# Two gates and a second norm's scale and shift, computed as column-tiled row products in a transformer block on Trainium2

## The chip, the cores and the metric

The kernel runs on one core of one Trainium2 chip. The metric is the device time of one execution, in microseconds (us). The engines are TensorE (PE, with its weight loads PEld), VectorE (DVE), ScalarE (ACT), GpSimd (POOL) and SyncE (SP), which issues nearly all DMAs.

## What is computed

The reference is a transformer block with adaptive layer norm. Six vectors of 1024 come out of one product of the conditioning vector `c` with `w_mod`; they scale, shift and gate an attention part (32 heads of 32, one shared key and value head) and a SwiGLU feed-forward part. There are 2048 tokens, D = 1024, F = 3584, all in bf16.

```python
mod = (_silu(c) @ w_mod).reshape(c.shape[0], 6, 1, -1)
sa, ca, ga, sb, cb, gb = (mod[:, 0], mod[:, 1], ..., mod[:, 5])
h = _layernorm(x) * (1 + ca) + sa
x = x + ga * A(h, wq, wk, wv, wo)     # attention, one k and v head for 32 q heads
h = _layernorm(x) * (1 + cb) + sb
x = x + gb * B(h, w1, w3, w2)         # (silu(h @ w1) * (h @ w3)) @ w2
```

The change is about the last four of the six vectors: `ga` (m = 2), `sb` (m = 3), `cb` (m = 4) and `gb` (m = 5). The first two are needed first and are computed by other code (L769), which stays.

## The kernel before

The kernel writes all its work as nodes of a graph (`G.add`, with the engine, what is read and written, an assumed duration and a priority). A planner, `schedule`, then walks through assumed time and lays down a fixed order of instructions for each engine. Where several kinds of work are possible, the table `CH` (number of the decision: alternative taken) says which comes first. Semaphore waits follow from the graph. Each engine works through its list strictly in order, so one instruction that waits holds up everything behind it on its engine.

The work runs in these stages.

1. The head: `x` is loaded in 16 tiles of 128 tokens, normalised on DVE (`ln`, L573 to L616) and transposed on PE (L630). The first norm's scale is multiplied into the weights: `kscale` and `qscale` (L798, L804, L807) make scaled key and query weights. `QCUT` cuts the query weights into three parts; the part k = 1 is scaled in eight pieces, of which every second goes to ACT when `QACT` is 1:

```python
if k == 1 and c % 2 < QACT:
    G.add("act", lambda e, c=c: e.activation(WQ[:, c, a:b], WO[:, c, a:b], ACT.Identity, ...   # L804
else:
    G.add("dve", lambda e, c=c: e.tensor_scalar(WQ[:, c, a:b], WO[:, c, a:b], ...              # L807
```

   The raw query weights lie in the buffer `WO` until they are scaled; then the output weights are loaded into it (L875). Key, value and query projections are `kproj` (L685, L692), `vproj` (L699, L702) and `qproj` (L709, copied out by L712).

2. Attention runs over eight blocks of 256 queries. In each, one unit of work is eight score matmuls (L969) of 32 rows each into half of PSUM (six banks, `SP`) and two exponentials on ACT of 128x1024 (L979). DVE sums the exponentials in trees (L996, L1002, L1012), PE multiplies them with V (L1035) and forms the denominators (L1062), DVE copies these out (L1074, L1083, L1086) and divides (L1092 to L1102).

3. After block 0, and then after each block, `post` does the output projection (L1167), the second norm, and the feed-forward: gate and up matmuls (L1208), tanh on ACT (L1216), products on DVE (L1213, L1223, L1228), the down projection (L1279, and L1250 in the last block). The feed-forward of one block is laid between the scores of the next. Its weights pass through a ring of six buffers in `WREG`, `HREG` and `X`.

The four vectors fall into stage 2, during the first block's attention, when the rest of the query projections is the only other work for PE. `vec(m, key, out)` loads the 1024 columns of `w_mod` that belong to m in four pieces of 512 KB (512 rows by 512 columns, L893) through three slots `WMS`, which lie in `WREG`. For each 128x128 tile it loads the weights into PE and multiplies by one column of the conditioning vector `SCT` (L899): 64 matmuls of one column for each vector. The vector thus comes out with one element per partition, which is what the second norm's scale and shift need (`MODC`, copied by L907). A gate is needed along the free axis in all partitions: `gate(m)` transposes it on PE (L914), copies it (L916), writes it to DRAM (L918) and reads it back broadcast to all partitions into `GBB` (L920). The first gate is then multiplied into the output weights (L926). The second gate goes into the same `GBB` and is used in the feed-forward.

After a few marks of time without work PE fills in with dummy matmuls (L1320, up to 250 us of planned time), which the planner adds.

Of the kernel before, what the change touches and what calls it, by code (L numbers as in the profile page):

```python
# [8 lines left out]
P = 128  # L9
# [4 lines left out]
LOOK = 0.5  # L14
LK = 0.6
LF = 0.5
CH = {2: 1, 24: 1, 25: 2, 82: 1, 136: 1, 142: 1, 147: 1, 188: 1, 202: 1, 210: 1, 211: 1, 232: 1, 242: 1, 374: 1,
      412: 1, 414: 1, 429: 1, 431: 1, 495: 1, 516: 1, 573: 1, 632: 1, 801: 2, 807: 1, 1116: 2, 1191: 1, 1204: 1,
      1208: 2, 1236: 1, 1333: 2, 1726: 2, 1801: 1, 1814: 1, 1818: 2, 1846: 1, 1943: 2, 2336: 2, 2411: 1, 2424: 1,
      2428: 2, 2456: 1, 2553: 2, 2946: 2, 3021: 1, 3034: 1, 3038: 2, 3066: 1, 3163: 2, 3556: 2, 3631: 1, 3655: 1,  # L20
      3669: 1, 3689: 1, 3778: 2, 3793: 1, 3802: 1, 4131: 1, 4166: 1, 4167: 1, 4183: 2, 4192: 3, 4238: 1, 4302: 1,
      4387: 1, 4394: 1, 4418: 1, 4429: 2, 4475: 1, 4490: 1, 4508: 2}


class Node:
# [390 lines left out]
def build(nc, x_in, wq_in, wk_in, wv_in, wo_in, w1_in, w3_in, w2_in, c_in, wmod_in, out, S, D, F):  # L416
# [51 lines left out]
    DSB = sb("DSB", [P, 2, QB], F32)  # L468
    ASB = XN[:, 2:4, :].rearrange("p a d -> p (a d)").bitcast(F32).rearrange("p (a q) -> p a q", a=4)
    SCT = sb("SCT", [P, NC], BF16)  # L470
    GC = sb("GC", [P, 2, NC], BF16)
    GR = sb("GR", [8, 2, P], BF16)
    gscr = nc.dram_tensor("gscr", [2, D], BF16, kind="Internal").ap()
    CROW = sb("CROW", [8, P], BF16)
    CT = sb("CT", [8, P], F32)
    SCR = sb("SCR", [8, P], BF16)
# [46 lines left out]
    def grp(allow=None):  # L523
        g = Group()
        g.allow = allow
        return g
# [16 lines left out]
    def dma(fn, key, reads=(), writes=(), nbytes=0, after=(), clear=()):  # L543
        return G.add("sp", fn, reads=reads, writes=writes, dur=0.06, dkey=key, nbytes=nbytes, after=after, clear=clear)
# [175 lines left out]
    ONPOOL = ()  # L720
    ME = True
    KP = 1
    QACT = 1
    TRP = 1
    EV = (("act",), ("act", "dve"), ("dve",), ("dve",))
    ORDER = ("x0", "x1", "x2", "x3", "x4", "x5", "a0", "a1", "x6", "a2", "a3", "x7", "a4", "a5", "a6", "a7", "q0",
# [38 lines left out]
    for h in (1, 0):  # L765
        for k in range(NC):
            def mm(e, k=k, g=gm[h], h=h):
                for j in range(NC):
                    i = e.matmul(PB[g.bank][:, j:j + 1], WM01[:, k, h * D + j * P:h * D + (j + 1) * P], SCT[:, k:k + 1],  # L769
                                 start=(k == 0 and j == 0), stop=True, skip_group_check=True)  # L770
                return i
# [108 lines left out]
        qproj(256, 256, f, (0, 1))  # L880

    def wms(i):
        return [("WMS", i)]
    nwm = [0]

    def vec(m, key, out):
        g = grp()
        for h in range(2):
            for kb in range(2):
                sl = nwm[0] % 3  # L890
                nwm[0] += 1
                c0 = m * D + h * 512
                dma(lambda e, kb=kb, c0=c0, sl=sl: e.dma_start(  # L893
                    WMS[:, sl], wmod_in[kb * 512:(kb + 1) * 512, c0:c0 + 512].rearrange("(c p) f -> p c f", p=P)),
                    ("wms", sl), writes=wms(sl), nbytes=P * 2048 * 2, after=[wo_load])
                for k in range(4):
                    def mm(e, kb=kb, h=h, sl=sl, g=g, k=k):
                        for j in range(4):
                            i = e.matmul(PB[g.bank][:, h * 4 + j:h * 4 + j + 1], WMS[:, sl, k, j * P:(j + 1) * P],  # L899
                                         SCT[:, kb * 4 + k:kb * 4 + k + 1],  # L900
                                         start=(h == 0 and kb == 0 and k == 0 and j == 0), stop=True,
                                         skip_group_check=True)
                        return i
                    G.add("pe", mm, reads=["SCT"] + wms(sl), dur=4 * 0.034, lat=0.2,
                          acq=g if (h == 0 and kb == 0 and k == 0) else None, groups=[(g, "w")], mode="F")
        a, b2 = {2: (1.0, 0.0), 3: (1.0, 0.0), 4: (1.0, 1.0), 5: (0.5, 0.0)}[m]
        G.add("dve", lambda e, g=g: e.tensor_scalar(out, PB[g.bank][:, 0:8], a, b2, ALU.mult, ALU.add),  # L907
              writes=[key], groups=[(g, "r")], dur=0.15, prio=4 if m in (3, 4) else 0)

    def gate(m):  # L910
        i = m // 3
        vec(m, ("GC", i), GC[:, i])
        g = grp()
        G.add("pe", lambda e, g=g, i=i: e.transpose(PBH[g.bank][0:8, 0:P], GC[:, i], IDENT[:]),  # L914
              reads=["IDENT", ("GC", i)], dur=0.07, lat=0.2, acq=g, groups=[(g, "w")], mode="F")
        G.add("dve", lambda e, g=g, i=i: e.tensor_copy(GR[:, i], PBH[g.bank][0:8, 0:P]), writes=[("GR", i)],  # L916
              groups=[(g, "r")], dur=0.2, prio=0)
        dma(lambda e, i=i: e.dma_start(gscr[i].rearrange("(k p) -> k p", p=P), GR[:, i]), ("gw", i), reads=[("GR", i)],  # L918
            writes=[("GSCR", i)], nbytes=2048)
        dma(lambda e, i=i: e.dma_start(GBB[:], gscr[i].unsqueeze(0).broadcast_to([P, D])), ("gr", i),  # L920
            reads=[("GSCR", i)], writes=[("GBB", 0), ("GBB", 1)], nbytes=P * D * 2)

    G.chain = GCH
    gate(2)
    for f in range(NC):
        G.add("dve", lambda e, f=f: e.tensor_tensor(WO[:, f, :], WO[:, f, :], GBB[:], ALU.mult),  # L926
              reads=["WO", ("GBB", 0), ("GBB", 1)], writes=[("WOG", f)], dur=dve_t(1024, 2), prio=6)
    for m in (3, 4):
        vec(m, ("MODC", m), MODC[:, m, :])
    gate(5)  # L930
    G.chain = 0
    for tb in range(1, NTB):
        for f in range(NC):
# [434 lines left out]
```

## Time and profile before

| | us |
|---|---|
| median of 4 runs | 1135.64 |
| lowest, highest | 1133.03, 1136.79 |
| the profiled execution, its own time | 1133.43 |
| the profiled execution, its span from first to last instruction | 1131.6 |

| engine | busy us | share of the span |
|---|---|---|
| PE | 1104.4 | 98% |
| DVE | 995.5 | 88% |
| ACT | 1020.1 | 90% |
| POOL | 36.7 | 3% |

| group of lines in the profile | count | mean ns of one |
|---|---|---|
| L979 exponential, ACT | 1024 | 1111 |
| L1216 tanh, ACT | 112 | 720 |
| L969 score matmul, PE | 4096 | 273 |
| L1035 product with V, PE | 4096 | 274 |

All durations in the document are those of one profiled execution. Neighbouring instructions of one engine overlap in the profile, since each is shown from its start to its result, so the distance from start to start is shorter than a duration. Busy time of PE is no proof that PE is at its limit: a matmul of 256 columns is shown with 273 ns, and the next can start 109 ns after it. The mean granted TensorE clock was 0.998 of full speed.

### The profile page before, as it was taken

How to read it: one execution, taken by the hardware profiler on the slowest of the kernel's cores; microseconds unless marked ns; L12 is line 12 of the kernel's file. 1: busy time of each engine (PE TensorE's matmuls, PEld its weight loads, DVE VectorE, ACT ScalarE, POOL GpSimd, SP SyncE). 2: the span in 40 equal slices, each digit the busy share in tenths (PEclk: the TensorE clock that was granted, in tenths of full speed). 3: DMA queues.
4: the chain of work that ended last, by engine and by line, in shares of the span. 5: the costliest groups of instructions: out<-in, count | busy, mean ns of one | idle time of the engine just before them, and what ended most of it. 6: DMA issues, size and time to landing. Idle time of an engine off the chain costs nothing.

```text
span 1131.6 us, 34956 instructions
## 1 busy us (share of the span) xinstructions
PE 1104.4 (98%) x15531; PEld 744.3 (66%) x15566; DVE 995.5 (88%) x1504; ACT 1020.1 (90%) x1167; POOL 36.7 (3%) x86
## 2 busy tenths in 40 slices
PE   7898999999999999999999999999999999999998
PEld 4564444767577757776677757776677757777883
DVE  6878899999989998999999998999999999997552
ACT  5999999999999999999999999999999999991110
POOL 3200000000000000000000000000000010000000
PEclk9999999999999999999999999999999999999999
DMA  9706203966596658766696649756785659656994
GB/s 332 230 25 188 76 1 88 285 192 176 142 259 195 168 163 217 213 185 178 147 258 184 182 123 261 206 170 173 170 249 171 178 140 271 191 166 182 295 309 142
DMA packets 378854, 211.58 MB, mean 187 GB/s; under 512 B 21840, under 2 KB 369488, under 8 KB 378704
## 3 DMA queue, kind: packets, MB, share of 16 engines
q1 hardware_dynamic: 376624, 209.22, 66.4%
q8 instruction: 122, 2.00, 0.8%
q10 hardware_dynamic: 2080, 0.13, 0.1%
q14 instruction: 28, 0.23, 0.1%
HBM read 201.98 MB, written 4.20 MB: 182 GB/s over the span
## 4 chain that ended last, share of the span: by engine, by line
PE 85%; ACT 8%; DVE 4%; SPq 1%; DMA 1%; issue 0%; POOL 0%; DVEq 0%
PE PB L1208 34%; PE PB L1279 14%; PE SP L969 13%; PE PB L1035 9%; ACT UREG L979 8%; PE PB L1167 4%; PE SP L1208 3%; PE PB L709 2%; PE SP L1279 2%; PE PB L1062 1%; PE PB L1250 1%; PE SP L1250 1%; DMA WO<-in_A_wq_dram 1%; SPq L751 1%; DVE UREG L996 1%; DVE UREG L1012 1%
## 5 line engine op out<-in xcount | busy, mean ns | idle before, releaser
L979 ACT ACTIVATE UREG<-SP 128x1024 bf16<-128x1024 f32 x1024 | 965.1, 1111 | 1.3 <-PE SP L969 0.7
L1002 DVE TENSOR_TENSOR UREG<-UREG 128x2048 bf16<-128x2048 bf16 x248 | 301.8, 1217 | 1.5 <-ACT UREG L979 0.3
L969 PE MATMUL SP<-QT,KT 32*128 32x256 bf16 x4096 | 203.8, 273 | 5.3 <-ACT UREG L979 3.6
L1208 PE MATMUL PB<-QT,WREG 128*128 128x256 bf16 x1648 | 206.8, 273 | 0.5 <-DVE GSB L1213 0.5
L1208 PEld LDWEIGHTS PB<-QT,WREG 128*128 128x128 bf16 x1648 | 150.4, 98 | 44.1 <-issue 27.8
L996 DVE TENSOR_TENSOR UREG<-UREG 128x2048 bf16<-128x2048 bf16 x124 | 151.0, 1218 | 12.9 <-ACT UREG L979 12.9
L969 PEld LDWEIGHTS SP<-QT,KT 32*128 32x128 bf16 x4096 | 60.7, 92 | 125.3 <-ACT UREG L979 79.1
L1035 PE MATMUL PB<-UREG,V 128*32 128x256 bf16 x4096 | 134.2, 274 | 1.7 <-ACT UREG L979 1.0
L1208 PE MATMUL PB<-QT,HREG 128*128 128x256 bf16 x1056 | 133.0, 273 | 0.0
L1216 ACT ACTIVATE WREG<-GSB 128x512 bf16<-128x512 bf16 x112 | 80.6, 720 | 45.1 <-DVE GSB L1213 45.1
L1035 PEld LDWEIGHTS PB<-UREG,V 128*32 128x32 bf16 x4096 | 98.2, 96 | 30.4 <-issue 22.6
L1208 PEld LDWEIGHTS PB<-QT,HREG 128*128 128x128 bf16 x1056 | 96.3, 98 | 28.1 <-issue 17.5
L1279 PE MATMUL PB<-WREG,HREG 128*128 128x256 bf16 x700 | 88.3, 273 | 0.0
L1279 PEld LDWEIGHTS PB<-WREG,HREG 128*128 128x128 bf16 x700 | 64.3, 98 | 19.3 <-issue 11.2
L1228 DVE SCALAR_TENSOR_TENSOR HREG<-WREG,HREG 128x512 bf16<-128x512 bf16 x112 | 76.2, 684 | 0.8
L1213 DVE CAST GSB<-PB 128x512 bf16<-128x512 f32 x104 | 71.0, 682 | 3.2 <-PE PB L1208 2.2
L1223 DVE TENSOR_TENSOR HREG<-GSB,PB 128x512 bf16<-128x512 bf16 x98 | 66.5, 679 | 4.5 <-PE PB L1208 3.7
L1208 PE MATMUL PB<-QT,X 128*128 128x256 bf16 x528 | 67.2, 273 | 0.0
L709 PE MATMUL PB<-HREG,WREG 128*128 128x512 bf16 (+1 forms) x297 | 62.3, 342 | 4.9 <-DVE QT L712 2.3
L1012 DVE TENSOR_TENSOR UREG<-UREG 128x2048 bf16<-128x2048 bf16 x52 | 63.3, 1218 | 0.0
L1279 PE MATMUL PB<-HREG 128*128 128x256 bf16 x476 | 61.1, 273 | 0.0
L1074 DVE COPY XN<-PB 128x256 f32<-128x256 f32 x64 | 27.0, 422 | 34.6 <-PE PB L1062 34.4
(146 smaller groups left out, 920.2 us busy)
## 6 DMA issues: line engine op xcount, KB each, us to landing
WREG<-in_B_w_dram SPq DMA_DIRECT2D x112, 512.0 KB, 5.1
HREG<-in_B_w_dram SPq DMA_DIRECT2D x74, 512.0 KB, 5.3
WREG<-in_B_w_dram SPq DMA_DIRECT2D x33, 896.0 KB, 5.2
X<-in_B_w_dram SPq DMA_DIRECT2D x38, 512.0 KB, 5.3
HREG<-in_B_w_dram SPq DMA_DIRECT2D x21, 896.0 KB, 5.1
X<-in_B_w_dram SPq DMA_DIRECT2D x10, 896.0 KB, 5.1
X<-in_A_x_dram SPq DMA_DIRECT2D x32, 256.0 KB, 5.7
WREG<-in_w_mod_dram SPq DMA_DIRECT2D x16, 512.0 KB, 5.0
```

Source lines behind the costliest of these rows:

```text
L709: g = mm_group(NC, lambda e, b, c: e.matmul(b[:, 0:n], WQ[:, c, f * P:(f + 1) * P], HT[:, c, sl], start=c == 0, stop=c == NC - 1), lambda ...
L969: r = e.matmul(SP[:, b, o:o + qn], KT[32 * gg:32 * gg + 32, kts[j] * P:(kts[j] + 1) * P], QT[32 * gg:32 * gg + 32, f, q0:q0 + qn], start=T ...
L979: G.add("act", lambda e, u=u, h0=h0, n=n, b0=b0, nb=nb: e.activation(U[:, u, h0 * W:(h0 + n) * W].rearrange("p (b w) -> p b w", b=nb), SP[ ...
L996: G.add("dve", lambda e, tr=tr, u=u, fu=first_u: e.tensor_tensor(TR[:, tr, 0:4 * W], U[:, fu, 0:4 * W], U[:, u, 0:4 * W], ALU.add), reads= ...
L1002: G.add("dve", lambda e, tr=tr, u=u: e.tensor_tensor(TR[:, tr, 0:4 * W], TR[:, tr, 0:4 * W], U[:, u, 0:4 * W], ALU.add), reads=[("TR", tr) ...
L1012: G.add("dve", lambda e, ta=ta, tb=tb: e.tensor_tensor(TR[:, ta, 0:4 * W], TR[:, ta, 0:4 * W], TR[:, tb, 0:4 * W], ALU.add), reads=[("TR", ...
L1035: r = e.matmul(PB[g.bank][32 * gg:32 * gg + 32, 0:qn], V[:, kt, :], U[:, pu, (gg * npk + j) * qn:(gg * npk + j + 1) * qn], start=w0 + n == ...
L1208: return e.matmul(bk[:, j * qn:(j + 1) * qn], w13[:, w, c, j * P:(j + 1) * P], QT[:, c, q0:q0 + qn], start=c == 0, stop=c == NC - 1)
L1213: G.add("dve", lambda e, g=g, b=b: e.tensor_copy(GS[b][:, 0:2 * qn], PB[g.bank][:, 0:2 * qn]), writes=[("GS", b)], groups=[(g, "r")], dur= ...
L1216: G.add("act", lambda e, b=b: e.activation(TB[b], GS[b], ACT.Tanh, scale=0.5), reads=[("GS", b)], writes=[("TB", b)], clear=alias("TB"), d ...
L1228: G.add("dve", lambda e, fp=fp, b=b: e.scalar_tensor_tensor(HHT[:, 2 * fp:2 * fp + 2, 0:qn], TB[b][:, 0:2 * qn].rearrange("p (j q) -> p j ...
L1279: G.add("pe", lambda e, g=g, j=j, fc=fc, hf=hf, first=first, w2s=w2s: e.matmul(PB[g.bank][:, j * 256:(j + 1) * 256], HHT[:, hf * NH + fc, ...
```

## The change

In the changed kernel the four vectors are computed with the roles of the operands exchanged. The conditioning column, repeated to 32 columns, is the stationary operand, and `w_mod` streams past it: each matmul has 256 columns of `w_mod`, and four of them stand side by side in PE's column groups (`tile_position=(0, 32 * gg)`), one for each quarter of the 1024 outputs. Eight row blocks are accumulated. The result is a row: output group gg lies in partitions 32 gg to 32 gg + 31, all equal. DVE reads 128x256 of it into the buffer `GSB` (bf16 for the gates, f32 for the scale and shift), four rows of it are written to DRAM, and the vector is read back: broadcast into `GBB` for a gate, one element per partition into `MODC` for scale and shift. The matmuls of a vector wait for all four of its row quarters. The quarters are loaded as three pieces of 512 KB into the `WMS` slots and two of 256 KB into a part of `QT` that is free at that time.

Two constants change as well: `QACT` becomes 0, so that all eight pieces of the query weights' part k = 1 are scaled on DVE, and the table `CH` is another one, so that the planned order differs.

```diff
-    GC = sb("GC", [P, 2, NC], BF16)
-    GR = sb("GR", [8, 2, P], BF16)
     gscr = nc.dram_tensor("gscr", [2, D], BF16, kind="Internal").ap()
+    mscr = nc.dram_tensor("mscr", [2, D], F32, kind="Internal").ap()
...
-    QACT = 1
+    QACT = 0
...
     def wms(i):
-        return [("WMS", i)]
-    nwm = [0]
-
-    def vec(m, key, out):
+        return [("WMS", i)] if i < 3 else KRAWK + KREPK
+
+    def wmk(i, k, gg):
+        if i < 3:
+            return WR[:, NC * D + i * 2048 + k * D + gg * 256:][:, 0:256]
+        return QT[:, 3 + 2 * k + gg // 2, S - 512 + gg % 2 * 256:][:, 0:256]
+
+    def vec(m):
+        a, b2 = {2: (1.0, 0.0), 3: (1.0, 0.0), 4: (1.0, 1.0), 5: (0.5, 0.0)}[m]
+        gt, i, hs = m in (2, 5), m // 3 if m in (2, 5) else m - 3, m % 2
+        row = GSB[:, hs * 512:hs * 512 + 256] if gt else GSB[:, hs * 512:(hs + 1) * 512].bitcast(F32)
+        scr = gscr if gt else mscr
+        for q in range(4):
+            src = wmod_in[q * 256:(q + 1) * 256, m * D:(m + 1) * D].rearrange("(c p) f -> p c f", p=P)
+            for k in range(1 if q < 3 else 2):
+                if q < 3:
+                    dst = WR[:, NC * D + q * 2048:][:, 0:2048].rearrange("p (c f) -> p c f", c=2)
+                    sk = src
+                else:
+                    dst = QT[:, 3 + 2 * k:5 + 2 * k, S - 512:S]
+                    sk = src[:, k].rearrange("p (h f) -> p h f", h=2)
+                dma(lambda e, src=sk, dst=dst: e.dma_start(dst, src), ("wms", q + k), writes=wms(q)[4 * k if q == 3 else 0:][:8],
+                    nbytes=P * 4096 // (1 + q // 3), after=[wo_load])
         g = grp()
...
+        for q in range(4):
+            def mm(e, g=g, q=q):
+                for k in range(2):
+                    for gg in range(4):
+                        n = e.matmul(PB[g.bank][32 * gg:32 * gg + 32, 0:256],
+                                     SCT[:, 2 * q + k:2 * q + k + 1].broadcast_to([P, 32]), wmk(q, k, gg),
+                                     start=q == 0 and k == 0, stop=q == 3 and k == 1, tile_position=(0, 32 * gg),
+                                     skip_group_check=True)
+                return n
+            G.add("pe", mm, reads=["SCT"] + [k for x in (range(4) if q == 0 else (q,)) for k in wms(x)],
+                  dur=512 / 2400.0 + 0.007, lat=0.2, acq=g if q == 0 else None, groups=[(g, "w")], mode="V", cls="V")
+        G.add("dve", lambda e, g=g: e.tensor_scalar(row, PB[g.bank][:, 0:256], a, b2, ALU.mult, ALU.add),
+              writes=[("GS", hs)], groups=[(g, "r")], dur=dve_t(256), prio=0)
+        dma(lambda e: e.dma_start(scr[i].rearrange("(g f) -> g f", f=256), row[0:P:32, :]), ("gw", m),
+            reads=[("GS", hs)], writes=[("GSCR", m)], nbytes=4096)
+        if gt:
+            dma(lambda e: e.dma_start(GBB[:], scr[i].unsqueeze(0).broadcast_to([P, D])), ("gr", m),
+                reads=[("GSCR", m)], writes=[("GBB", 0), ("GBB", 1)], nbytes=P * D * 2)
+        else:
+            dma(lambda e: e.dma_start(MODC[:, m, :], scr[i].rearrange("(c p) -> p c", p=P),
+                                      allow_slow_non_contiguous=True), ("gr", m),
+                reads=[("GSCR", m)], writes=[("MODC", m)], nbytes=P * 4096)
...
-    gate(2)
+    vec(2)
...
     for m in (3, 4):
-        vec(m, ("MODC", m), MODC[:, m, :])
-    gate(5)
+        vec(m)
+    vec(5)
```

In the changed kernel the new matmuls are L911, the DVE reads L918, the writes L920 and the read-backs L923 and L926; lines of the attention and of what follows it stand 7 further down than before (L969 becomes L976).

## The prediction

> **What bounds the kernel now.** I read the page first, then the busy time in stretches of 25 us, then ScalarE's waits, then the timelines around two places. PE has 98% on the page and most of the chain of waits, which invites the reading that every saved PE microsecond counts. The line of the softmax exponentials says otherwise.
>
> ```profile
> span 1131.6 us, 34956 instructions
> L979 ACT ACTIVATE UREG<-SP 128x1024 bf16<-128x1024 f32 x1024 | 965.1, 1111 | 1.3 <-PE SP L969 0.7
> ```
>
> 1024 exponentials, and in front of them 1.3 us of idle time in the whole run. The stretches, with columns PE, PEld, DVE, ACT, POOL:
>
> ```profile
> 28.00:53.00 25.00, 22.10 (x453) 14.34 (x452) 23.07 (x60) 25.00 (x28) 6.76 (x16) 1.00 0.67 217
> ...
> 78.00:103.00 25.00, 21.87 (x364) 11.38 (x365) 20.18 (x32) 24.27 (x28) 0.00 (x0) 0.93 0.47 143
> 103.00:128.00 25.00, 21.92 (x420) 11.87 (x425) 23.54 (x36) 25.00 (x29) 0.00 (x0) 1.00 0.47 152
> ...
> 1003.00:1028.00 25.00, 25.00 (x384) 19.01 (x382) 23.14 (x34) 20.38 (x25) 0.00 (x0) 1.00 0.69 192
> ```
>
> ACT is full from 28 us to its last exponential at 1023; one stretch, 78 to 103, lacks 0.73 us. PE has 3 us of idle time in each stretch around the vectors (78 to 128). One attention block of 125.20 us, exponentials first, tanh (L1216) second:
>
> ```profile
> 339.88:465.08 125.20, 120.98 (x129) 1.00 0.70 190
> ```
> ```profile
> 339.88:465.08 125.20, 10.25 (x14) 1.00 0.70 190
> ```
>
> Neighbours overlap, so starts count: 36 exponentials fill 33.19 us, 0.92 us each, and a tanh in between adds 0.52; 128 x 0.92 + 14 x 0.52 = 125.0. So ACT sets the pace. I call the eight score matmuls of L969 and their two exponentials a **step**: 1.84 us, 512 of them. The span is: first exponential at 27.75, 995.6 us of ACT to 1023.4, 108.2 us of PE after it (last block's projection and feed-forward). A change here pays only if it moves the first exponential, takes a hole out of ACT, or shortens the end.
>
> The two places where ACT is not simply full. The start, on ACT, DVE and PE:
>
> ```profile
> 25.71 2.13 ACT L804 ACTIVATE WREG<-WO,MODC 128x384 bf16<-128x384 bf16 x4
> 27.75 33.19 ACT L979 ACTIVATE UREG<-SP 128x1024 bf16<-128x1024 f32 x36
> ```
> ```profile
> 25.71 1.01 DVE L807 TENSOR_SCALAR WREG<-WO,MODC 128x384 bf16<-128x384 bf16 x4 [0.70 <-DMA WO<-in_A_wq_dram]
> 26.64 0.48 DVE L712 TENSOR_SCALAR QT<-SP,BIA 128x256 bf16<-128x256 f32 x1
> ```
> ```profile
> 27.17 0.40 PE L969 MATMUL SP<-QT,KT 32*128 32x256 bf16 x8 [0.33 <-DVE QT L712]
> ```
>
> The first scores wait for L712, which stands behind four L807; their results are there at 27.57, and L804 holds ACT to about the same moment. The hole, on PE, ACT and in the granted clock (the third number from the end):
>
> ```profile
> 86.08 0.75 PE L899 MATMUL PB<-SCT,WREG 128*128 128x1 bf16 x24
> ...
> 88.10 2.31 PE L709 MATMUL PB<-HREG,WREG 128*128 128x512 bf16 x5
> 90.34 0.61 PE L969 MATMUL SP<-QT,KT 32*128 32x256 bf16 x8
> ```
> ```profile
> 91.01 39.59 ACT L979 ACTIVATE UREG<-SP 128x1024 bf16<-128x1024 f32 x43 [0.73 <-PE SP L969]
> ```
> ```profile
> 88.00:89.00 1.00, 1.00 (x7) 0.35 (x4) 0.00 (x0) 1.00 (x2) 0.00 (x0) 0.50 1.06 373
> ```
>
> After two runs of 24 one-column matmuls the clock is 0.50 from about 87.6 to 91.0, L709 takes twice its time, and the scores come 0.73 us late.
>
> [...] The trace has 24 weight loads of L899 in 0.68 us, 28 ns each. [...] at 91.26, 32 matmuls of L1035 of 256 columns take 0.88 us to the next line's start, a quarter of 32 x 0.109. [...]
>
> **The change part by part.** The order of instructions of both programs can be compared without times; I count its steps.
>
> 1. PE, vectors: 256 matmuls of L899 at 28 ns (7.2 us) and two transposes go; 4 x 32 four-group matmuls come, 4 x 0.88 = 3.5 us. PE saves nearly 4 us between 85 and 123 us. On the path: 0, because PE waits for ACT there. The projections of L709 that follow move up instead. The first gate-and-up matmul moves from step 90 to 86, but the order gives this lead back: by step 192 both programs have the same feed-forward work done, and from step 203 to the end the PE order is identical. So the end keeps its 108.2 us.
> 2. The hole: with L899 gone, the half clock at 88 should go: **-0.7 us**. Bounds: -0.73, or 0 if the gate falls elsewhere.
> 3. QACT 1 to 0: ACT loses four L804 (2.13 us), DVE gets four more L807. In the new DVE order L712 stands behind one L807 instead of four, the other seven after it. That L807 still waits for its weights at 25.71. L712 moves 3 x 0.2325 = 0.70 us forward, and the 0.1 us by which L804 outlasted the scores goes: first exponential about 27.0, **-0.8 us**. Its next debtor is the query of step 5, due at 27.0 + 4 x 1.84 = 34.3. DVE, added up from the same rows: L807, L712, two L807, the key copy (0.38), five L807, one statistic (0.60), the 512-wide key copy (0.65), four statistics, two bias copies (0.16), two statistics: L712 starts at 33.3, scores end at 34.3. Just in time; 0 taken, 0 to +0.5 as bounds.
> 4. DVE, vectors: four reads of 128x256 at 0.42 us (as L1074) for four L907 (0.163) and two L916 (0.18): +0.7 us; with the L807 +1.6. Cover: DVE's 19 us of idle time in 28 to 178. Without it, L712 and so the scores would come late by as much.
> 5. SP: 20 loads for 16, and two more write and read pairs, 8 issues of 0.3 to 0.5 us. The load of WO (L875) now follows scalings that stand later in DVE's order: I add up about 49 us for 41.15. Its first reader is the gate scaling after step 31 (84 us). What is queued behind it is late next: two quarters, then x and w1 loads, then the rest; 4.25 MB at the 370 GB/s of the load stretches is 11.5 us, and the last half quarter waits for the one before it, about 63 us. The first new matmul comes after step 23, 67.5 us.
> 6. Later vectors: every quarter waits for the previous vector's matmuls, and these stand 8 steps = 14.7 us apart (steps 23, 31, 39, 47). On SP: three quarters and half of the fourth; then the row write, which waits for DVE; then the second half, which waits for the first half to land. 0.5 MB lands in 3.5 us at best, 1.4 of it transfer, so 2.1 fixed: 1.75 MB/370 + 2.1 = 6.8, then 0.4 + 0.7 + 2.1 = 3.2: 10 us of 14.7. Cost 0; if this cover of 4 us goes, PE stands in order before the matmul with all scores behind it.
> 7. The read back of MODC in 1024 pieces of 4 bytes: no row shows it; below zero is excluded, as it replaces a direct write. Its reader is at step 82, some 60 us after the last such read starts; even 10 us cost nothing.
>
> Sum: -0.8 - 0.7 = -1.5 us; the profiled execution had 1133.43, so 1131.9. It lies 2.2 below the median of 1135.64; the same gain there gives 1134.1.
>
> **The rivals.** (a) The half clock bites oftener in the other runs: they spread over 1133.03 to 1136.79[...]. If all of the 2.2 us is that, all of it goes too: 1131.9. Against it: no view shows the cause of the spread. (b) The four-step lead reaches the end: -4 x 1.84 = -7.4 more, 1126.7. Against it: the identical order from step 203 and a full ACT. (c) The gate falls at steps 83 to 85 of the new order, where the scores have 12 transposes beside them and little else: 0.7 us comes back, 1134.8. (d) **Slower:** the chain of part 6 takes 18 us instead of 10, by slower landing (L893 had up to 8.1 us) or by the DVE read in its middle. The six score banks let PE be half a step, 0.9 us, ahead, so each of three vectors costs 18 - 14.7 - 0.9 = 2.4: +7.2 - 1.5, 1141.3. It decides from a chain of 15.6 us; it passes the unmeasurable from 17.3.
>
> **How the numbers follow.** A measurement of this kernel tells about 0.3% (3.4 us) from no change: faster means under 1132.2, slower over 1139.0. Likeliest 0.55 (1134.1), (a) 0.15, (b) 0.05, (c) 0.12, (d) 0.13. Faster: (a), (b) and 0.03 of the likeliest, 0.23; slower: (d) and 0.02, 0.15; same 0.62. Range 1130.8 to 1138.6: leaves out (b) and most of (d), and takes in the runs' own spread.
>
> **What would show it.** Right: first exponential near 27.0; no granted clock under 1.00 at 80 to 100; ACT idle under 0.3 us up to 1022; about 108.2 us after the last exponential; the new matmuls 0.9 us per vector with no DMA wait ahead. Wrong: PE waits named DMA before the new matmuls, ACT idle that PE's scores end, or an end shorter than 105 us.

## The result: slower by 0.14%, where 0.14% faster was expected

The changed kernel takes 1135.87 us in the median (38 runs, 1131.88 to 1139.64), the kernel before, beside it, 1134.45 us (59 runs, 1132.14 to 1137.09). The ratio is 1.0014, 95% interval [1.0008, 1.0019]: about 1.6 us slower. The profiled execution of the changed kernel took 1134.96 us for a span of 1133.2; that of before took 1133.43 for 1131.6. The two profiles differ by 1.5 us, the medians by 1.4, so the profiles can be compared line by line.

From the page of the changed kernel, the span and the line of the exponentials (its last part: idle time of ACT in front of the group, and what ended most of it):

```profile
span 1133.2 us, 34714 instructions
L986 ACT ACTIVATE UREG<-SP 128x1024 bf16<-128x1024 f32 x1024 | 969.2, 1127 | 4.9 <-PE SP L976 4.1
```

The 1.3 us of idle time before have become 4.9, and 4.1 of them end when scores arrive from PE. The stretches say where (columns PE, PEld, DVE, ACT, POOL, then granted clock, DMA share, GB/s):

```profile
53.00:78.00 25.00, 22.62 (x454) 14.34 (x453) 14.72 (x25) 22.39 (x25) 0.00 (x0) 0.93 0.74 247
78.00:103.00 25.00, 22.20 (x332) 11.44 (x331) 23.51 (x38) 25.00 (x28) 0.00 (x0) 1.00 0.43 134
```

The stretch 78 to 103, which lacked 0.73 us of ACT before, is full and at full clock, as predicted. The stretch 53 to 78, full before, now lacks 2.61 us, and the clock there is 0.93. Of the stretches beside them, 28 to 53 and 103 to 128 have ACT at 24.87 and 24.99 of 25.

**The start came as predicted.** ACT, DVE and PE of the changed kernel around the first exponential:

```profile
26.59 38.96 ACT L986 ACTIVATE UREG<-SP 128x1024 bf16<-128x1024 f32 x42 [1.49 <-PE SP L976]
```
```profile
25.37 0.32 DVE L807 TENSOR_SCALAR WREG<-WO,MODC 128x384 bf16<-128x384 bf16 x1 [0.71 <-DMA WO<-in_A_wq_dram]
25.61 0.48 DVE L712 TENSOR_SCALAR QT<-SP,BIA 128x256 bf16<-128x256 f32 x1
```
```profile
26.14 0.40 PE L976 MATMUL SP<-QT,KT 32*128 32x256 bf16 x8 [0.30 <-DVE QT L712]
```

From the landing of the weights (start of the first L807) to the first exponential it is 26.59 - 25.37 = 1.22 us, and was 27.75 - 25.71 = 2.04. That is the forecast 0.8 us. The weights also landed 0.34 us earlier, though SP issues the loads of the head in the same order in both kernels; no run shows why.

**A new hole.** PE and ACT of the changed kernel, where the stretch 53 to 78 breaks:

```profile
62.85 0.40 PE L976 MATMUL SP<-QT,KT 32*128 32x256 bf16 x8
63.18 0.32 PE L699 MATMUL PB<-WKS,HREG 128*128 128x32 bf16 x6
65.26 0.21 PE L699 MATMUL PB<-WKS,HREG 128*128 128x32 bf16 x2 [1.76 <-issue]
65.33 1.48 PE L709 MATMUL PB<-HREG,WREG 128*128 128x256 bf16 x10
66.74 0.61 PE L976 MATMUL SP<-QT,KT 32*128 32x256 bf16 x8
```
```profile
67.41 1.94 ACT L986 ACTIVATE UREG<-SP 128x1024 bf16<-128x1024 f32 x2 [1.86 <-PE SP L976]
70.10 30.36 ACT L986 ACTIVATE UREG<-SP 128x1024 bf16<-128x1024 f32 x33 [0.75 <-PE SP L976]
```

PE stops in the middle of a group of eight value-projection matmuls (L699), after the sixth, for 1.76 us. The releaser is "issue": nothing that the profile shows was waited for, no semaphore, no buffer. The next scores come 2 us late. From 66.2 to 69.6 us the clock is at half (0.50 in 67 to 69): the six L709 that start at 67.29 take 1.38 us to the next line's start, where e1_xlate below, at full clock, has 0.76. So the scores after that are late once more.

What PE lacked was instructions, as e1_xlate and e2_burst below bear out. The list of DMA queues has one queue, q8, of kind "instruction" (121 packets, 1.98 MB, so 16 KB each), which brings PE's program. (That it is PE's is a count: its 121 pieces stand against 30847 matmuls and weight loads of PE on the page, 255 for each piece; no other engine has more than 1506 instructions.) In the changed kernel none came in 60 to 62 us, and one in 62 to 64 (share of 16 engines in the last column):

```profile
q1 hardware_dynamic: 691, 0.63, 106.6%
q8 instruction: 1, 0.02, 3.7%
```

A narrower window puts its start between 62.7 and 62.9 us; 3.7% of 16 engines for 2 us is 1.2 us of transfer, so it landed at about 64.0, and PE went on at 65.26. Queue q1, the data, fills the engines at that time (119.3% in 60 to 62 us). SP's queue shows whose data this is, first one line of before, then the changed kernel:

```profile
41.15 0.38 SPq L875 DMA_DIRECT2D WO<-in_A_wo_dram  x1
```
```profile
48.09 0.38 SPq L875 DMA_DIRECT2D WO<-in_A_wo_dram  x1
...
50.63 7.20 SPq L1205 DMA_DIRECT2D X<-in_B_w_dram  x2
57.88 3.28 SPq L904 DMA_DIRECT2D WREG<-in_w_mod_dram  x1
```

The load of WO goes out at 48.09 us instead of 41.15, as forecast (about 49), and everything behind it moves too. Before, the data had landed by about 60 us, and no packet moved in 62 to 64. Now the burst runs on to about 65 us, and just there PE works through 64 value-projection matmuls of 32 columns, each with its own weight load: 48 of them take 1.33 us from their start to the next line's, so PE uses 96 instructions in that time. At this pace a piece of 255 lasts it about 3.5 us (an estimate), against 9.4 us in the mean of the run (1133 us by 121 pieces).

Counted out on the starts of the exponentials (numbered from 0), the difference of the two profiles (after minus before) is: landing of the weights -0.34 us, start -0.82, given back by exponential 40 +0.27, hole at 64 to 70 us +2.82, hole at 88 gone -0.86 (all that is left of the difference up to exponential 80), and +0.43 lost, in the net, between exponentials 80 and 512. The sum is +1.50, which stays constant from exponential 512 to the last.

### The profile page after: what moved, and what is told of

It is laid out like the page before. It is cut to its first block, busy times and chain, and to the rows that moved or that the text cites. A ratio compares the mean times of both kernels' runs of the same rounds, so it can differ in the third digit from the quotient of the medians.

```text
span 1133.2 us, 34714 instructions
## 1 busy us (share of the span) xinstructions
PE 1103.8 (97%) x15407; PEld 740.2 (65%) x15440; DVE 996.7 (88%) x1506; ACT 1018.7 (90%) x1163; POOL 39.4 (3%) x86
## 2 busy tenths in 40 slices
DMA packets 377925, 211.58 MB, mean 187 GB/s; under 512 B 23968, under 2 KB 365488, under 8 KB 377776
## 3 DMA queue, kind: packets, MB, share of 16 engines
q8 instruction: 121, 1.98, 0.7%
## 4 chain that ended last, share of the span: by engine, by line
PE 77%; ACT 16%; DVE 4%; SPq 1%; DMA 1%; issue 1%; DVEq 0%
PE PB L1215 28%; ACT UREG L986 15%; PE PB L1286 14%; PE SP L976 12%; PE PB L1042 8%; PE PB L1174 4%; PE SP L1215 3%; PE PB L709 2%; PE SP L1286 2%; PE PB L1069 1%; PE PB L1257 1%; PE SP L1257 1%; DMA WO<-in_A_wq_dram 1%; SPq L751 1%; ACT WREG L1223 1%; DVE UREG L1003 1%
## 5 line engine op out<-in xcount | busy, mean ns | idle before, releaser
L976 PE MATMUL SP<-QT,KT 32*128 32x256 bf16 x4096 | 203.6, 273 | 9.6 <-ACT UREG L986 8.2
L976 PEld LDWEIGHTS SP<-QT,KT 32*128 32x128 bf16 x4096 | 60.7, 92 | 131.9 <-ACT UREG L986 89.6
L1223 ACT ACTIVATE WREG<-GSB 128x512 bf16<-128x512 bf16 x112 | 84.1, 751 | 45.1 <-DVE GSB L1220 45.1
L709 PE MATMUL PB<-HREG,WREG 128*128 128x512 bf16 (+1 forms) x300 | 62.7, 342 | 3.6 <-DVE QT L712 1.6
L1215 PEld LDWEIGHTS PB<-QT,X 128*128 128x128 bf16 x528 | 48.4, 98 | 13.5 <-issue 8.4
```

Source lines behind the costliest of these rows:

```text
L709: g = mm_group(NC, lambda e, b, c: e.matmul(b[:, 0:n], WQ[:, c, f * P:(f + 1) * P], HT[:, c, sl], start=c == 0, stop=c == NC - 1), lambda ...
L976: r = e.matmul(SP[:, b, o:o + qn], KT[32 * gg:32 * gg + 32, kts[j] * P:(kts[j] + 1) * P], QT[32 * gg:32 * gg + 32, f, q0:q0 + qn], start=T ...
L1215: return e.matmul(bk[:, j * qn:(j + 1) * qn], w13[:, w, c, j * P:(j + 1) * P], QT[:, c, q0:q0 + qn], start=c == 0, stop=c == NC - 1)
L1223: G.add("act", lambda e, b=b: e.activation(TB[b], GS[b], ACT.Tanh, scale=0.5), reads=[("GS", b)], writes=[("TB", b)], clear=alias("TB"), d ...
```

## The experiments

**Theory F**: the fetch of PE's instructions waits behind the load burst. **Rival P**: the stop, or the loss, comes from the new order of PE's work. **Theory G**: the half clock at 88 us before (the "gate" of the prediction and of e4_warm's expectation) came from the one-column matmuls L899.

### e1_xlate: the changed kernel with less in the burst

The planned order of SP is edited after the planner has run; nothing else changes.

```diff
+    place(XL, "sp", last_vec)      # the two loads of w1 into X (L1205), moved on SP behind the last vector's read-back
```

> Changed kernel; only the two early w1 loads into X (1 MB) are moved on SP's queue from between the first vector's loads to behind the last vector's read back. Orders of PE, DVE and ACT are untouched. Theory F (fetch): the 2 us stop of PE at 63 us in the middle of a run of L699 comes from PE's next 16 KB of instructions, fetched late behind the load burst of 48 to 65 us; with 1 MB less the burst ends near 60 us and the stop goes: ACT's two holes of 1.9 and 0.75 us vanish, 2.0 to 3.0 us less than the changed kernel, about 1132 to 1133 (0.998 of before). Rival P (PE order): the stop belongs to the denser order of PE, which is the same here: nothing changes, about 1135.9.

Measured: 1134.17 us (1132.14 to 1136.73), against 1134.77 of before beside it; ratio 0.9999 [0.9989, 1.0009]. The loss against before is gone. The median did not reach the 1132 to 1133 that was expected; the profiled execution, at full clock throughout, did (1132.14), and is 2.82 us ahead of the changed kernel's at the last exponential. PE of e1_xlate at the same place, then its stretch 53 to 78 us:

```profile
62.86 0.40 PE L978 MATMUL SP<-QT,KT 32*128 32x256 bf16 x8
63.19 0.36 PE L699 MATMUL PB<-WKS,HREG 128*128 128x32 bf16 x8
63.40 1.26 PE L709 MATMUL PB<-HREG,WREG 128*128 128x256 bf16 x10
```
```profile
53.00:78.00 25.00, 24.12 (x485) 15.37 (x482) 17.32 (x28) 25.00 (x29) 0.00 (x0) 1.00 0.59 209
```

PE's program is the same one and had reached the same instruction within 0.01 us; the group of eight now runs through. The data queue, in 60 to 62 us, and the fetch in it:

```profile
q1 hardware_dynamic: 154, 0.24, 33.2%
q8 instruction: 1, 0.02, 3.4%
```

A narrower window puts its start between 60.6 and 60.8 us. It was due at the same point of the same program, so the burst had held it up by some 2 us. Rival P falls: the order of PE is unchanged. The margin is small here too: PE comes to the instruction at which the changed kernel stopped 2.7 us after this fetch has begun, and in the changed kernel PE goes on 2.5 us after it has begun.

### e2_burst: the kernel before with the burst 19 us later

```diff
+    wo_load.deps.append(kp_last)   # the load of WO (L875) waits for the last key projection
```

> Kernel before; only the load of WO (L875) has to wait for the last key projection (about 58 us for 41), and the 3 MB behind it on SP's queue with it. No order is changed. Theory F: the burst now lies at 58 to 71 us over the same dense L699 run (step 19 to 21), PE stops for 1 to 2 us between 61 and 68 us with no semaphore as cause, the clock falls to 0.5 after it, ACT has a hole of 1 to 3 us there: 1135.5 to 1137.5. Rival P: the order of PE is that of before, which has no stop there: no hole, 1134.5.

WO goes out at 60.0 us instead of 41.15.

Measured: 1138.18 us (1137.06 to 1141.09), ratio 1.0029 [1.0018, 1.0041]. PE of before at this place, then of e2_burst, which has the vectors and the order of before:

```profile
64.08 0.36 PE L699 MATMUL PB<-WKS,HREG 128*128 128x32 bf16 x8
```
```profile
66.25 0.26 PE L699 MATMUL PB<-WKS,HREG 128*128 128x32 bf16 x4
68.88 0.27 PE L699 MATMUL PB<-WKS,HREG 128*128 128x32 bf16 x4 [2.36 <-issue]
```

The same stop, in the same kind of group, 2.36 us long, without one line of the new vector code. ACT waits 5.9 us for scores in this execution, 3.5 us of it at once. The DMA queues in 66 to 68 us:

```profile
q1 hardware_dynamic: 399, 0.78, 102.3%
q8 instruction: 1, 0.02, 3.0%
```

The fetch began between 66.4 and 66.5 us, as PE ran dry. Together with e1_xlate this shows theory F from both sides: moving the burst onto this place makes the stop, moving it off removes it. The time is longer than the 1135.5 to 1137.5 that were expected, and not all of it is the stop: the profile also has half clock at 21 to 28 us, with a first exponential 2.15 us later than before, and for 3.4 us each from 69, 93 and 117 us.

A count tells what kind of place this is: the stop comes after 1982, 1985 and 1985 recorded instructions of PE in after, e8_after2 (below) and e2_burst, though e2_burst has another order of PE. It belongs to a number of instructions, as the edge of a piece of program would, and not to one line.

### e4_warm: the kernel before with PE kept at work among the one-column matmuls

```diff
+                        if k % 2:
+                            i = e.matmul(PB[g.bank][:, 256:512], IDENT[:], IDENT[:].unsqueeze(1).broadcast_to([P, 2, P]),
+                                         start=False, stop=True, skip_group_check=True)
```

> Kernel before with 32 dummy matmuls of 256 columns among the 256 one-column matmuls L899 (one after every eighth, into unused columns of the same bank). Theory G (gate): the half clock at 88 us comes from the one-column matmuls; with work between them it goes, ACT's hole of 0.73 us at 90 us too: 0.5 to 1.0 us shorter, 1133.7, and runs nearer to each other. Rival: the gate fell there by the waits of PE on ACT and DVE, dummy work changes nothing, or its 3.4 us make scores late: 1134.5 to 1135.

Measured: 1134.09 us (1132.70 to 1135.08), ratio 0.9993 [0.9984, 1.0002]. The stretch 78 to 103 us of e4_warm:

```profile
78.00:103.00 25.00, 22.85 (x389) 12.73 (x387) 21.06 (x34) 24.95 (x29) 0.00 (x0) 1.00 0.42 128
```

It is at full clock, ACT busy 24.95 of 25, where before had 0.93 and 24.27. (This profile has half clock in the head, from 20.7 to 27.5 us.) This is one execution, but the other profiles agree: e2_burst and e3_start, which have L899 as it was, have half clock from 93 and 117 and from 91 and 114 us, and none of the seven profiles with the new vectors has any between 70 and 180 us. The hole at 88 goes when PE gets dense work among L899, as theory G says; what that brings, some 0.7 us, is at the edge of what the interval can tell from nothing.

### e3_start: the start alone, put into the kernel before

```diff
-                G.add("act", lambda e, c=c: e.activation(WQ[:, c, a:b], WO[:, c, a:b], ACT.Identity, ...
+                n.eng, n.fn = "dve", n.alt       # the four L804 go to DVE; its next 20 instructions in the changed kernel's order
```

> Kernel before; only the head part of the change: the four L804 of ACT become L807 on DVE, in the changed kernel's order (one scaling, L712, two scalings, key copy, five scalings). Theory: first exponential 0.8 us earlier after the landing of the weights (2.04 us becomes 1.2 us), the time 0.4 to 0.8 us shorter, 1133.8. Rival: the query of step 5 comes late on DVE by as much as is won, the time is as before, 1134.5.

Measured: 1137.09 us (1134.83 to 1139.11), ratio 1.0023 [1.0016, 1.0030]; a miss, and not for a reason that tells the theories apart. The rest of PE's order is that of the kernel before, which fits other times of DVE: value and query copies come late, and ACT waits 0.66, 0.40 and 1.29 us for scores after six, ten and twelve exponentials. The clock was at half four times in the profile, from 22, 39, 91 and 114 us. The start had to be tried in the changed kernel, the other way round.

### e5_qback: e1_xlate with the four scalings back on ACT

```diff
+    for n in QA:                   # the four even pieces of qscale(1)
+        G.order["dve"].remove(n)
+        n.eng, n.fn = "act", n.alt
+    ao[at:at] = QA                 # ahead of the first exponential
```

> This is e1_xlate (the changed kernel with the two early w1 loads behind the last vector's read-back) with one thing put back: the four even 128x384 scalings of the query weights are on ACT again, ahead of the first exp, as in the kernel before. Theory H (the start is worth what the prediction said): the first exp comes 2.0 us after the landing of the weights instead of 1.2 us, nothing later makes up for it, and the end of the exps is 0.8 us later than in e1_xlate: median about 1135.0 us. Rival G (the early start is given back within a few steps, because steps 1 and 3 wait for scores that are late whatever ACT does; e1_xlate has gaps of 1.03 and 1.14 us there instead of 0.92): the first exp is 0.8 us later, but those two gaps close, and from step 8 on the exps are only 0.5 us later: median about 1134.7 us. Either way no stop of PE near 64 us.

Measured: 1134.16 us (1132.31 to 1136.30), ratio 0.9994 [0.9987, 1.0000]: the median of e1_xlate, 1134.17. ACT of e5_qback at the start:

```profile
25.40 2.13 ACT L812 ACTIVATE WREG<-WO,MODC 128x384 bf16<-128x384 bf16 x4 [0.26 <-DMA WO<-in_A_wq_dram]
27.44 32.99 ACT L993 ACTIVATE UREG<-SP 128x1024 bf16<-128x1024 f32 x36
```

The first exponential is 0.85 us later than in e1_xlate, but exponential 8 is only 0.39 later and the last one 0.37. Rival G holds in the profiles: steps 1 and 2 of e1_xlate (numbered from 0) wait for scores that stand behind other PE work, so half of the early start runs into them. The 0.8 us of the start are worth 0.4 us there. The medians don't show it: both theories expected a later one, 1135.0 and 1134.7 us.

### e6_fill and e7_xlate2: where the spread of the runs comes from

e6_fill is e1_xlate with a longer dummy fill; e7_xlate2 is e1_xlate itself.

```diff
+    h.fn = warm(h.know[0], h.know[1] + 3)   # three more dummy matmuls at 18.2 us
```

> e1_xlate with three more 512-column dummy matmuls (0.66 us in all) at 18.2 us, ahead of PE's wait for the next part of w_mod, so that PE is idle less at 20 to 21 us. Theory S (the spread of the runs of e1_xlate, 1132.1 to 1136.7 us at granted clocks of 1.000 to 0.992, is mostly half clock in the head, which the profiles of three experiments show at 20 to 28 us after such an idle stretch and which puts the first exp 1.7 to 2.1 us later): the slow runs go, mean clock of most runs 0.997 or more, median 1132.5 to 1133.5 us. Rival (the half clock of e1_xlate's runs lies elsewhere, between 30 and 300 us): median stays at 1134.2 us within 0.5, with the same spread. Second rival: the dummies delay the transposes behind them and with them the start by up to 0.66 us, median 1134.8 us.

> e1_xlate once more, for a second profile: its first one was an execution at full clock (1132.1 us), its median is 1134.2. Theory S: this execution is 1.5 to 2.5 us slower than the first and its profile shows half clock at 20 to 28 us, the first exp about 28.5 us instead of 26.6, and the rest as in the first. Rival: first exp at 26.6 us and half clock somewhere between 30 and 300 us. In either case no idle PE of more than 1 us at 60 to 66 us.

Measured: e6_fill 1134.10 us (1132.61 to 1136.37), ratio 0.9995 [0.9987, 1.0004]; e7_xlate2 1134.15 us (1132.40 to 1136.47), ratio 0.9997 [0.9987, 1.0008]. Theory S fell in both: the head is at full clock and the first exponential on time. The half clock lies at 34 to 41 us. ACT of e7_xlate2 there, and the busy time and clock of e7_xlate2 in two windows:

```profile
26.68 9.62 ACT L988 ACTIVATE UREG<-SP 128x1024 bf16<-128x1024 f32 x10 [1.47 <-PE SP L978]
36.80 1.94 ACT L988 ACTIVATE UREG<-SP 128x1024 bf16<-128x1024 f32 x2 [0.49 <-PE SP L978]
39.16 21.47 ACT L988 ACTIVATE UREG<-SP 128x1024 bf16<-128x1024 f32 x23 [0.43 <-PE SP L978]
```
```profile
33.00:34.00 1.00, 0.47 (x9) 0.20 (x10) 1.00 (x3) 1.00 (x2) 0.00 (x0) 1.00 0.03 9
...
35.00:41.00 6.00, 6.00 (x103) 3.71 (x105) 4.59 (x13) 5.08 (x7) 3.42 (x8) 0.50 0.38 121
```

Nearly 7 us at half clock, after stretches in which PE had half its time free (busy 0.47 of 1 us in 33 to 34), cost about 1.4 us of ACT. The first profile of e1_xlate has the same idle stretches (PE busy 0.49 in 33 to 34 us) and full clock throughout.

A count over all eleven profiles, which no run put to the test, suggests why one execution is hit and the other is not. Within each profile the changes of clock lie whole multiples of 3.413 us apart (e8_after2: from 186.52 to 316.23, 38 times; before and after have one stretch of half clock each behind the head, 87.65 to 91.06 and 66.21 to 69.62 us), so each profile from 28 us on can be divided into such windows. A matmul is counted for the time in which its columns stream, 109 ns for 256 columns (the distance of two starts), and matmuls that run side by side are counted once. Each of the 14 stretches of half clock there follows a window in which PE streams for 40% of the time or less; among some 3,500 windows only three others are that low, at 35 to 39%. Busy time does not tell: PE is busy for 85% of the window before the hole at 88 (84.24 to 87.65 us), which streams for 28%, since the one-column matmuls fill the profile and hardly stream (the 24 from 86.08 us are shown with 0.75 us and stream, by this count, for 0.01). And the windows lie differently in each execution: one of e7_xlate2 runs from 31.01 to 34.42 and takes in both idle stretches (37%), while e1_xlate's are cut at 32.52 and have 44% or more.

### e8_after2: the changed kernel once more

> The changed kernel once more, for a second profile. Theory F (the fetch of PE's next instructions is queued behind the load burst in every execution): again a stop of PE of 1.5 to 2.5 us with no semaphore between 62 and 67 us, half clock for some 3.4 us after it, and 3 us lost on ACT there; 1134.9 to 1137 us. Rival (the stop was an accident of the one execution): no such stop, and 1132 us at full clock or the loss elsewhere.

Measured: 1136.71 us (1134.70 to 1140.37), ratio 1.0023 [1.0014, 1.0031]. PE of e8_after2 at the place of the stop:

```profile
63.15 0.31 PE L699 MATMUL PB<-WKS,HREG 128*128 128x32 bf16 x6
65.49 0.21 PE L699 MATMUL PB<-WKS,HREG 128*128 128x32 bf16 x2 [2.03 <-issue]
```

The stop is there again, at the same matmul, 2.03 us long. This time no half clock follows it, and by exponential 80 the loss against e1_xlate is 1.74 us, not 2.83. The half clock comes at 183 us and at 316 us instead; the first costs 0.6 us, and the second, which follows PE's idle time before it (busy 0.69, 0.40 and 0.00 of 1 us in 313 to 316), 1.1 us. Beside e7_xlate2, on the same chip, the changed kernel is 2.56 us slower: that is the price of the burst's place, in medians, with whatever half clock it brings.

### e9_warm: e5_qback with dummy matmuls in PE's idle stretches at 31 to 39 us

```diff
+            if i == 4 * NC - 1:
+                for _ in range({0: 3, 1: 5}.get(tb, 0)):
+                    r = e.matmul(b[:, 256:512], IDENT[:], IDENT[:].unsqueeze(1).broadcast_to([P, 2, P]), start=False, stop=True,
+                                 skip_group_check=True)
...
+            for _ in range(6):
+                r = e.matmul(PB[g.bank][:, 256:512], IDENT[:], IDENT[:].unsqueeze(1).broadcast_to([P, 2, P]), start=False,
+                             stop=True, skip_group_check=True)
```

> e5_qback (the changed kernel with the two early w1 loads late and the four scalings back on ACT) plus 14 dummy 256-column matmuls, 6, 3 and 5 of them behind the three groups of PE after which it is idle for 0.91, 0.30 and 0.70 us at 31 to 39 us. Theory S2 (the slower runs of e1_xlate, e5_qback and e6_fill are those in which the clock halves for one or two times 3.4 us at 34 to 41 us, as the profiles of e6_fill and e7_xlate2 show, and PE's idle stretches just before draw it): nearly all runs at a granted clock of 0.998 or more, median 1132.4 to 1133.2 us, where e5_qback has 6 of 21 runs there and a median of 1134.2. Rival (the half clock of those runs comes from the wait for w_mod at 19 to 21 us or from the idle PE at 312 to 315 us): clocks and median as in e5_qback, within 0.4 us. Second rival: the dummies hold up the scores behind them, exps 3 to 12 come up to 0.5 us late and the best run is 1132.8 us instead of 1132.3.

Measured: 1134.95 us (1133.16 to 1136.91), before beside it 1134.93; ratio 0.9994 [0.9986, 1.0003]. The profile has full clock from 14 to 50 us, and half clock at 183 us, after a stretch with PE busy 2.56 of 4 us, and at 316 us. Seven of the 14 runs have a clock of 0.998 or more, where e5_qback had 6 of 21, but at 0.999 or more it is two of 14 against 6 of 21, and the median is no better: theory S2 fails for the time, and that the dummies keep the clock up at 34 to 41 us rests on this one profile. The other idle stretches are still there. A small stop is back as well, again after 1982 recorded instructions: the 14 dummies and their weight loads are 28 instructions more, and it stands 28 instructions earlier in the program than in after. PE of e9_warm:

```profile
63.82 0.40 PE L991 MATMUL SP<-QT,KT 32*128 32x256 bf16 x8 [0.68 <-issue]
```

By exponential 40 the lead of 0.16 us over e5_qback has become a lag of 0.42. That is a part of the 0.85 us by which its best run, 1133.16 us, is slower than e5_qback's, measured on another chip. No run filled the idle stretches before 183 and 316 us.

No version tried is measurably better than the kernel before. The lowest ratios are 0.9993 (e4_warm) and 0.9994 (e5_qback, e9_warm), with intervals that reach 1.0000 or more.

## Why the prediction was wrong

It said -1.5 us and got about +1.6. The sign was lost in one step; the others held in kind, two with other sizes. That 1135.87 us lies within its range is luck: the range was wide for the spread of the runs, not for this loss. Its 1134.1 also started from the median of four runs, 1135.64, where 59 runs give 1134.45.

- **ACT sets the pace**: right. The difference of the two profiles is one of exponential starts, and the part after the last exponential has kept its length: 1133.2 - 1024.9 = 108.3 us, before 108.2.
- **Part 5, SP: the step that failed.** It had the facts right (WO at 49 us, a burst of several MB, its end past 60 us) and asked only who waits for the *data*: "The first new matmul comes after step 23, 67.5 us", and so cost nothing. It did not ask who else uses the DMA engines in those microseconds. PE's own program comes over them (q8 in the same list, 0.7% of the 16 engines over the run). So the cost that it put at nothing was, in the profiles, 2.82 us (stop and half clock behind it) or 1.74 us (stop alone), and in medians 2.56 (e8_after2 against e7_xlate2). Most fetches cost PE nothing that shows: of the 121 fetches of the changed kernel's profile, 52 began after 2 us in which the data alone took 100% or more of the 16 engines, and yet no other "issue" wait of PE is longer than 0.3 us. At this one fetch PE stops, for 1.76, 2.03 and 2.36 us in the three profiles with a full data queue at that fetch, and for 0.68 in e9_warm, whose queue was at 58%. What sets these profiles apart is the time from the fetch's start to PE's need of it. In these four PE goes on 2.45 to 2.64 us after the start; in the seven profiles without a stop it comes to the instruction of that number 2.57 to 3.99 us after.
- **Part 3, the start**: 0.82 us from landing to exponential, as worked out, but 0.4 us at the end (e5_qback). The term missed that steps 1 and 2 had slack before and have none with an earlier start. The debtor that it named, the query of step 5, was in time.
- **Part 2, the hole at 88**: gone; worth 0.86 us in the profiles. But other places have half clock: the profiles of the changed kernel, e6_fill, e7_xlate2 and e9_warm have it at 34 to 41, 66, 183 or 316 us. This is rival (c) in kind, at places that it did not name, and it goes with (a), full clock in all runs, not coming. That the half clock falls at other places in other executions, the profiles of one kernel now show: 66 us in after, 183 and 316 us in e8_after2.
- **Part 1, PE**: the lead was given back, as read from the order: the exponentials run in parallel from number 512 on. "0 on the path" was nearly right: between exponentials 80 and 512 the profile loses 0.43 us in the net, in part where scores beside feed-forward work come 0.1 us late each. No run isolates it. The new order also leaves PE idle at 312 to 316 us (busy 2.66 of 4 us in after, 4.00 in before), where the half clock struck in two profiles.
- **Parts 4, 6 and 7**: right. ACT is full in the stretches of the vectors (25.00 and 24.99 of 25), so DVE's extra reads hold up no scores. The new matmuls L911 never wait for a DMA (ahead of them stand 1.5 us of "issue" and 0.4 of L712), so the chain of loads stays within the eight steps between two vectors, and rival (d) had the sign by another mechanism. The read-backs in small pieces show in the page's count of packets under 512 B (23968, before 21840); each read-back into `MODC` landed 3.4 to 3.7 us after its issue, 70 us ahead of its first reader (182.2 us).

Without the burst at that place the same change is worth nothing measurable (e1_xlate and e7_xlate2: 0.9999 and 0.9997, intervals across 1), though its one profile at full clock is 1.3 us ahead of that of before (1132.14 against 1133.43).

## What to carry to other kernels

When a change moves a large load, lay its new interval over PE's timeline and ask not only when its data are due, but how dense in instructions PE is meanwhile: here 48 small matmuls with a weight load each took 96 instructions of PE in 1.33 us, and the next piece of program came late while the data filled the 16 DMA engines (106.6% in 62 to 64 us), which stopped PE for 1.76 us. A stop of PE inside a group of equal matmuls, marked "issue", is looked up in the list of DMA queues, under the kind "instruction", not in the semaphores. Here 3.4 us of half clock followed a stretch in which PE was busy with one-column matmuls (before, 88 us: PE streamed for 28% of the 3.4 us ahead), and nearly 7 us followed one in which PE had half its time free (e7_xlate2: 37%), though not in the other profile of that kernel (e1_xlate): one profile at full clock does not clear such a place. And a microsecond gained at the start counts only after the next few steps have been checked for slack: here 0.8 us were worth 0.4.

## What was not expected of the hardware

- A fetch of 16 KB took 1.0 to 1.2 us with the data engines busy (after, e2_burst) and with them mostly free (e1_xlate, 33%); what differed was its start. PE went on 1.3 to 1.5 us after it had landed (64.0 to 65.26 in after, 64.0 to 65.49 in e8_after2).
- The half clock does not follow every stop: after 1.76 us without work it came (after), after 2.03 us it did not (e8_after2). By the count of windows above PE streams for 35% of the window with the stop in after (62.79 to 66.21 us) and for 39% in e8_after2 (63.64 to 67.05), which is one of the three exceptions, so the 40% of that count is no sharp limit. Among 38 runs of the changed kernel the two at a mean clock of 0.999 or more took 1131.88 and 1132.32 us, the 18 at 0.997 and 0.998 took 1133.96 to 1136.07. The two are as quick as e1_xlate at full clock (1132.14), so the stop itself was probably absent too; there is no profile of such a run.
